# A recurrence with a two-layer MoE on one core: the second product of seven steps as seven block products, the MoE weights in fp16, and one decay sum moved to VectorE

## Chip, core and metric

The kernel runs on one core of a Trainium2 chip. The metric is device time in microseconds of one launch. The kernel before took 183.21 us (median of three runs, 183.01 to 183.66). Engines are called PE (TensorE), DVE (VectorE), ACT (ScalarE), POOL (GpSimd) and SP (SyncE, which only issues transfers).

## What is computed

For 4 batches and 8 heads of width 48, a state of 48 x 48 runs over 768 tokens. The outputs of all heads side by side are a row of 384 for each of 3072 tokens, and that row goes through two products with a squared relu between them.

```python
for t in range(S):                                   # per batch and head
    cur = outer(u * k[t], v[t])
    y[t] = r[t] @ (state + cur)
    state = w[t][:, None] * state + outer(k[t], v[t])
x = y laid out as [3072, 384]
h = x @ w_in                                         # 384 x 2048
g = maximum(h, 0) ** 2
out = g @ w_out                                      # 2048 x 384
```

All inputs and the output are fp32.

## The kernel before

**Tiling.** The work is 12 steps, three to a batch, of 256 tokens each; a partition holds two neighbouring tokens. A step has an attention part and a MoE part. In the attention part the decay is summed within chunks of 128 tokens in the log domain, the state is carried from chunk to chunk, and the products are bf16 matmuls. In the MoE part the step's 256 tokens go through the first product in 8 groups of 2 x 128 hidden units, and then through the second product in two halves of 128 tokens (`c`), each 16 matmuls of 384 columns that accumulate over the 2048 hidden units in one PSUM bank.

**The order.** Nothing is scheduled by a compiler. `ORDER` (from line 17) is a list of words, each the call of a small function; instructions are issued to their engines in the order of the words, and each engine works through its own list in order, held back by semaphores where data is not ready or a buffer not free. A word is `name.step...`; `:n` names a PSUM bank and `=A`, `=V` or `=G` the engine (ACT, DVE, POOL). PE, DVE, ACT, POOL and SP each have one queue. SP issues all loads, stores and DMA transposes.

**The words of a step**, with the line of their main instruction:

- `ld.s.x`: loads of w, r, k, v (L180); `ld.g.i` and `ld.g.o`: quarters of w_in (L188) and w_out (L193); `cast.i.g`, `cast.o.g`: their casts to bf16 (L200).
- `ww_`, `rw_`, `kw_`: products of two SBUF tiles (L267, L279, L283) on POOL or DVE. `lw_`: the logarithm (L271, ACT).
- `cum_`: the decay sums by matmuls: four of 2 columns (L311), the exclusive sum (L313) and the negated inclusive sum (L314), 384 columns each. `exp_` and `ac_` (L318, L325, ACT) take exponentials of them in PSUM.
- `rd_`: r and k times their decays (L332, DVE). They are transposed either on PE (`tr_`, L341, with the copies `rkt_`, L345) or by DMA (`dtr_`, L348).
- `p_` (L365), `pm_` (mask, L376, DVE), `su_` (L387), `ts_` (L395, L397), `sn_` (the state, L401, POOL), and `y_`, `yq_`, `yc_` (L411): the attention's products.
- `ku_`, `qp_` (L286, L291, POOL), `q_` (L294, DVE), `vq_` (L297, POOL): the term of u.
- `ysb_` (L449): eviction of y. Its transposes are `yt_` on PE (L457) with the copy `xt_` (L461), or `dyt_` by DMA (L464).
- `m1_` (L474): a group of the first product, 6 matmuls of 256 columns into one of four banks. `rl_` (relu, L481 on ACT, L483 on DVE) evicts it; `sq_` (L489 on ACT, L491 on DVE) squares four blocks of 128 hidden units in place.
- `m2_.s.c.q` (L497): a quarter of a token half of the second product, 4 matmuls of 384 columns. `os_` (L503 on ACT, L505 on DVE) evicts a half, scaled; `store` (L509).
- `warm_.n.b` (L513): n matmuls of 512 columns on zeros.

**Memory.** PSUM has two double banks (`att`) for the attention and four single banks (`one`) for the MoE and the transposes. SBUF buffers are handed on by counting uses (`buf`, line 159).

Of the kernel before, what the change touches and what calls it, by code (L numbers as in the profile page):

```python
# [29 lines left out]
cast.o.1=G rl_.1.3=V ww_.3=V vq_.2 m2_.0.1.0:3 p_.2.0:1 p_.2.1:0 sq_.1.1=A lw_.3 pm_.2.1 m2_.1.1.0:0 sq_.1.2=A  # L30
m2_.1.0.0:2 sn_.2.0 qp_.3 pm_.2.0 q_.3 rw_.3=V m2_.0.0.1 m2_.1.1.1 m2_.1.0.1 m2_.0.1.1 cum_.3:0 y_.2:1 ww_.4=G kw_.3=G
v_.3=G sq_.1.3=A cast.o.2=A yc_.2 sq_.0.2=A yq_.2 m2_.1.1.2 kw_.4=G ysb_.2=V cast.o.3=A ac_.3 exp_.3 m2_.1.0.2
m2_.0.0.2 m2_.0.0.3 m2_.1.1.3 rd_.3.0 rd_.3.1 os_.0.0=A ld.5.v ld.6.w ld.5.k lw_.4 os_.1.1=A m2_.1.0.3 os_.1.0=V
yt_.2:1 cum_.4:1 tr_.3.0:0 su_.3:0 xt_.2=A rw_.4=G tr_.3.1:2 m2_.0.1.2 m1_.2.0:1 ts_.3.0=V rkt_.3.0=V sn_.3.0 ww_.5=G
ac_.4 exp_.4 ld.7.w store.0.0 rd_.4.0 v_.4=G ku_.4 rkt_.3.1=A m2_.0.1.3 m1_.2.6:2 m1_.2.3:0 ts_.3.1=V rd_.4.1 p_.3.1:1
p_.3.0:0 vq_.3 dtr_.4.1 os_.0.1=A qp_.4 sn_.3.1 v_.5=G kw_.5=G rl_.2.3=A lw_.5 rl_.2.0=A pm_.3.1 m1_.2.1:3 m1_.2.2:0
m1_.2.5:1 pm_.3.0 su_.4:1 y_.3:0 rl_.2.1=A sq_.2.0=A dtr_.4.0 rl_.2.5=A yc_.3 yq_.3 rl_.2.6=V ysb_.3=A rl_.2.2=V
m1_.2.7:3 m1_.2.4:1 cum_.5:0 sq_.2.1=A rl_.2.7=V yt_.3:2 ts_.4.0=V rl_.2.4=V ac_.5 xt_.3=A sn_.4.0 q_.4 rw_.5=V ku_.5
sq_.2.2=A m2_.2.0.0:0 exp_.5 m2_.2.0.1 m2_.2.1.0:2 rd_.5.0 m2_.2.1.1 rd_.5.1 m2_.2.1.2 m1_.3.7:1 dtr_.5.0 m1_.3.1:3
sq_.2.3=A rl_.3.1=A dtr_.5.1 qp_.5 store.1.1 m2_.2.1.3 ts_.4.1=V p_.4.1:0 p_.4.0:1 rl_.3.7=V os_.2.1=V m1_.3.3:1  # L40
m2_.2.0.2 ld.6.r ld.6.k ld.7.r vq_.4 sn_.4.1 pm_.4.0 ww_.6=G ww_.7=G pm_.4.1 m1_.3.2:2 m1_.3.0:3 su_.5:1 y_.4:0
ts_.5.0=V q_.5 rl_.3.0=V yc_.4 ld.7.k store.1.0 ld.6.v ld.8.w yq_.4 p_.5.0:1 pm_.5.0 rl_.3.3=A rl_.3.2=A sq_.3.1=A
ysb_.4=A m1_.3.5:2 m2_.2.0.3 ku_.6 vq_.5 yt_.4:1 m1_.3.4:3 p_.5.1:1 xt_.4=V lw_.7 cum_.7:0 rl_.3.5=V os_.2.0=A lw_.6
pm_.5.1 m1_.3.6:0 m1_.4.3:1 rw_.7=V rl_.3.4=A exp_.7 sq_.3.0=A kw_.7=G sn_.5.0 cum_.6:1 m1_.4.1:3 rl_.4.3=A rl_.4.1=A
kw_.6=G rw_.6=G m1_.4.0:2 m1_.4.5:1 rl_.3.6=A m2_.3.1.0:3 m2_.3.0.0:0 exp_.6 sq_.3.2=A rl_.4.5=A sq_.3.3=A rl_.4.0=V
rd_.7.0 m2_.3.0.1 m2_.3.1.1 rd_.7.1 m2_.3.0.2 rd_.6.0 m1_.4.4:1 ww_.8=G qp_.6 rd_.6.1 ac_.7 ld.8.r ld.7.v store.2.1
dtr_.6.0 dtr_.6.1 ld.11.w ac_.6 m2_.3.0.3 m1_.4.2:2 v_.6=A v_.7=A su_.6:1 y_.5:0 yc_.5 yq_.5 q_.6 m2_.3.1.2 ysb_.5=A
ts_.6.0=A m2_.3.1.3 os_.3.1=A os_.3.0=V rl_.4.4=V rl_.4.2=V ld.9.w ku_.7 vq_.6 sn_.6.0 yt_.5:1 ld.8.k store.3.0 ld.8.v
rw_.8=V ts_.6.1=V xt_.5=A qp_.7 m1_.4.7:0 m1_.4.6:3 m1_.5.7:2 sq_.4.2=A rl_.4.6=A rl_.4.7=A rl_.5.7=V p_.6.1:1
p_.6.0:0 m1_.5.0:1 m1_.5.1:3 pm_.6.1 m1_.5.5:0 m1_.5.4:2 pm_.6.0 rl_.5.0=V lw_.8 sq_.4.0=A rl_.5.1=A sq_.4.3=A  # L50
rl_.5.5=A y_.6:1 su_.7:0 store.0.1 ld.9.k sq_.4.1=V rl_.5.4=A sn_.6.1 kw_.8=V q_.7 dtr_.7.0 yc_.6 yq_.6 m2_.4.0.0:3
m1_.5.6:2 m1_.5.3:0 m1_.5.2:1 ysb_.6=A dyt_.6 rl_.5.6=V m2_.4.1.0:2 dtr_.7.1 rl_.5.2=A v_.8=A ld.9.r ld.10.w store.3.1
ts_.7.0=V sn_.7.0 rl_.5.3=V ww_.9=V m2_.4.1.1 cum_.8:1 m2_.4.0.1 ac_.8 lw_.9 exp_.8 m2_.4.0.2 ku_.9 sq_.5.0=A
# [36 lines left out]
def kernel(  # L90
# [39 lines left out]
    def bf16_bank(i):  # L130
        return one[i][:].bitcast(BF16)
# [434 lines left out]
```

## Time and profile before

| | |
|---|---|
| median of 3 runs | 183.21 us |
| the profiled execution | 183.09 us, its span 181.3 us |
| PE busy | 174.1 us (96%), 2293 matmuls |
| DVE busy | 127.1 us (70%) |
| ACT busy | 120.0 us (66%) |
| POOL busy | 110.8 us (61%) |
| first product (L474) | 576 matmuls, 71.2 us busy |
| second product (L497) | 384 matmuls, 68.9 us busy |
| chain that ended last, by engine | PE 86% |

The profile is of one execution. Its span runs from the first to the last instruction; the 1.8 us between span and time lie around it. A matmul's row gives its duration from issue to its end, and matmuls overlap: what one costs in a stream is the distance between starts, which the chain of work shows (so many of a line in so many microseconds). In the views a group is a line of the code with its engine and operation, what it writes and reads, the number of instructions, and the mean duration in nanoseconds; "idle before" is how long the engine stood still ahead of them, and who ended it.

### The profile page before, as it was taken

To read this page: it belongs to the slowest core of one execution; us is meant where nothing else is said; L and a number is where in the kernel's file an instruction comes from. 1 tells how busy PE (TensorE), PEld (TensorE's weight loads), DVE (VectorE), ACT (ScalarE), POOL (GpSimd) and SP (SyncE) were. 2 spreads that over 40 slices of the span, in tenths; PEclk is the share of its full clock that TensorE was granted. 3 is DMA by queue.
4 is the path that set the end of the run, shared out by engine and by line. 5 is a ranking of instruction groups with operands and counts; after the bars stand their busy time and mean duration, and the time that the engine had idled before them with its cause. 6 is when DMAs were issued, how large, how long until landed. Compare 5 with 4: busy or idle time off the path is not lost.

```text
span 181.3 us, 5434 instructions
## 1 busy us (share of the span) xinstructions
PE 174.1 (96%) x2293; PEld 125.1 (69%) x2294; DVE 127.1 (70%) x176; ACT 120.0 (66%) x191; POOL 110.8 (61%) x104
## 2 busy tenths in 40 slices
PE   7978899999999999999999999999999999999992
PEld 2355689766787787777777778777666777777661
DVE  5499958947787889776967969287996718327431
ACT  5779798999788568959949384747870366528001
POOL 6389989977899977999059960999555010000000
PEclk9999999999999999999999999999999999999999
DMA  5999999998999599979999559983659821302023
GB/s 149 325 352 395 334 235 356 353 343 205 309 241 190 102 236 302 288 179 262 289 109 254 108 118 245 239 233 115 34 130 145 192 47 43 90 0 87 4 87 130
DMA packets 78810, 35.61 MB, mean 196 GB/s; under 512 B 72129, under 2 KB 77250, under 8 KB 78786
## 3 DMA queue, kind: packets, MB, share of 16 engines
q1 hardware_dynamic: 78786, 35.27, 77.6%
q8 instruction: 18, 0.29, 0.7%
q14 instruction: 6, 0.05, 0.1%
HBM read 25.17 MB, written 4.72 MB: 165 GB/s over the span
## 4 chain that ended last, share of the span: by engine, by line
PE 86%; DMA 5%; SPq 5%; issue 1%; ACT 1%
PE one L497 35%; PE one L474 34%; PE att L411 7%; DMA w_st_b<-in_moe_w_in_dram 5%; SPq L180 3%; PE att L365 3%; PE att L387 2%; SPq L188 1%; PE one L341 1%; PE att L313 1%; PE one L457 1%; PE att L314 1%; SPq L208 1%; PE att L311 0%; ACT gt_b L481 0%
## 5 line engine op out<-in xcount | busy, mean ns | idle before, releaser
L474 PE MATMUL one<-xT_b,wi_sb 128*128 128x256 bf16 x576 | 71.2, 273 | 0.7 <-ACT gt_b L481 0.5
L497 PE MATMUL one<-wo_sb,gt_b 128*128 128x384 bf16 x384 | 68.9, 326 | 0.0
L474 PEld LDWEIGHTS <-wi_sb 128*128 128x128 bf16 x576 | 55.3, 98 | 11.7 <-issue 0.9
L497 PEld LDWEIGHTS <-gt_b 128*128 128x128 bf16 x384 | 36.7, 98 | 21.7 <-ACT gt_b L489 0.2
L481 ACT ACTIVATE gt_b<-one 128x512 f16<-128x512 f32 x51 | 29.9, 596 | 24.6 <-PE one L474 24.0
L483 DVE TENSOR_SCALAR gt_b<-one 128x512 f16<-128x512 f32 x45 | 30.3, 685 | 17.0 <-PE one L474 15.7
L489 ACT ACTIVATE gt_b<-gt_b 128x1024 bf16<-128x1024 f16 x38 | 39.4, 1054 | 0.9 <-DVE gt_b L483 0.7
L401 POOL TENSOR_TENSOR S_b<-t_b,ac_buf 128x384 bf16<-128x384 f32 x20 | 17.3, 864 | 23.9 <-DVE t_b L397 17.0
L376 DVE TENSOR_TENSOR pmT_b<-att,mask 128x1024 bf16<-128x1024 f32 x22 | 26.0, 1216 | 6.2 <-PE att L365 6.2
L286 POOL TENSOR_TENSOR ku_b<-k_b,u_bc 128x768 f32<-128x768 f32 x12 | 22.8, 1910 | 3.0 <-DMA k_b<-in_k_dram 2.3
L291 POOL TENSOR_TENSOR ku_b<-ku_b,r_b 128x768 f32<-128x768 f32 x12 | 21.8, 1814 | 1.2 <-DMA r_b<-in_r_dram 1.2
L297 POOL TENSOR_TENSOR vq_b<-v_b,q_b 128x768 bf16<-128x768 f32 x12 | 18.1, 1506 | 0.4 <-DVE q_b L294 0.3
L503 ACT ACTIVATE w_st_b<-one 128x384 f32<-128x384 f32 x12 | 5.9, 490 | 16.5 <-PE one L497 16.5
L294 DVE TENSOR_REDUCE q_b<-ku_b 128x16 f32<-128x768 f32 x12 | 11.3, 946 | 4.5 <-POOL ku_b L291 4.5
L332 DVE TENSOR_TENSOR rdec_buf<-r_b,att 128x768 bf16<-128x768 f32 x12 | 11.3, 949 | 3.9 <-ACT att L318 3.8
L505 DVE TENSOR_SCALAR w_st_b<-one 128x384 f32<-128x384 f32 x12 | 6.6, 552 | 8.2 <-PE one L497 7.5
L449 ACT CAST y_sb_b<-att 128x768 bf16<-128x768 f32 x8 | 6.4, 799 | 8.0 <-PE att L411 7.8
L332 DVE TENSOR_TENSOR rdec_buf<-k_b,att 128x768 bf16<-128x768 f32 x12 | 11.3, 948 | 0.5 <-ACT att L318 0.4
L279 POOL TENSOR_TENSOR r_b<-r_b,w_b 128x384 f32<-128x384 f32 x8 | 8.1, 1014 | 3.4 <-DMA r_b<-in_r_dram 3.4
L397 DVE TENSOR_TENSOR t_b<-S_b,att 128x384 f32<-128x384 bf16 x16 | 8.8, 547 | 1.7 <-PE att L387 0.9
L318 ACT ACTIVATE att<-att 128x768 f32<-128x768 f32 x12 | 9.6, 800 | 0.5 <-PE att L314 0.3
L513 PE MATMUL one<-warm 128*128 128x512 bf16 x23 | 8.1, 490 | 1.2 <-DVE warm L235 1.2
(71 smaller groups left out, 180.0 us busy)
## 6 DMA issues: line engine op xcount, KB each, us to landing
w_b<-in_w_dram SPq DMA_DIRECT2D x12, 384.0 KB, 5.1
r_b<-in_r_dram SPq DMA_DIRECT2D x12, 384.0 KB, 5.0
k_b<-in_k_dram SPq DMA_DIRECT2D x12, 384.0 KB, 6.0
v_b<-in_v_dram SPq DMA_DIRECT2D x12, 384.0 KB, 5.2
out_dram<-w_st_b SPq DMA_DIRECT2D x24, 192.0 KB, 2.3
w_st_b<-in_moe_w_in_dram SPq DMA_DIRECT2D x4, 768.0 KB, 9.6
w_st_b<-in_moe_w_out_dram SPq DMA_DIRECT2D x4, 768.0 KB, 8.2
rkT_b<-rdec_buf SPq DMA_TRANSPOSE x16, 3.6
```

The source lines that it names most:

```text
L286: nc.gpsimd.tensor_mul(buf("ku", s)[:], buf("k", s)[:, :, 1:3, :], u_bc[:, :, None, :].to_broadcast([C, H, 2, D]))
L291: nc.gpsimd.tensor_mul(ku[:], ku[:], buf("r", s)[:, :, 0:2, :])
L297: nc.gpsimd.tensor_mul(buf("vq", s)[:].rearrange("p j h d -> p h j d"), buf("v", s)[:], buf("q", s)[:, :, :, None].to_broadcast([C, H, 2, D]))
L332: nc.vector.tensor_mul(rdec[:, i, :, :, 0:D], x.rearrange("p h j d -> p j h d"), cs[:, i, 0:DM].rearrange("p (h d) -> p h d", h=H)[:, None ...
L376: nc.vector.tensor_mul(pmT, ps_p[:].rearrange("p e (a x) -> p (e a) x", a=2), mk.to_broadcast([C, 4, 2 * C]))
L401: nc.gpsimd.tensor_mul(buf("S", s + c, 1 - c)[:], buf("t", s, c)[:].rearrange("p (a e d) -> p a e d", a=HP, e=2), tiles["a_c", s][:, :, c, ...
L411: nc.tensor.matmul(ps_y[rows, c, cols], lhsT, rhs, start=fresh, stop=True, skip_group_check=True)
L474: nc.tensor.matmul(ps1[:, j, :], wi_sb[:, n // 4, kk, n % 4 * 128:(n % 4 + 1) * 128], xT[:, :, kk, :], start=(kk == 0), stop=(kk == KT - 1))
L481: nc.scalar.activation(rl, m1, AF.Relu, scale=RS)
L483: nc.vector.tensor_scalar(out=rl, in0=m1, scalar1=RS, scalar2=0.0, op0=ALU.mult, op1=ALU.max)
L489: nc.scalar.activation(gt, rl, AF.Square)
L497: nc.tensor.matmul(m2, gt[:, n, c * C:(c + 1) * C], wo_sb[:, n, :], start=(n == 0), stop=(n == NT - 1))
```

## The change

The second product of steps 4 to 10 is done by a scheme of the Strassen and Winograd kind. The two token halves (`c`), the even and odd blocks of hidden units (`k`) and the two halves of the 384 output columns make eight block products of 8 matmuls with 192 columns. Seven products of sums replace them: `sw_` forms four sums of blocks of the squared activations for each half of the hidden units (eight instructions of 128 x 512 elements a step), `tw_` forms four sums of weight blocks once, `pw_` are the seven products, and `cx_` and `ow_` evict and combine them (three and four instructions of 192 columns a step, in place of two `os_`). Two of the sums are written over the activations they no longer need; the others and the weight sums lie in buffers that the loads of the weights have left. In a bank `wx`, products 1, 6, 7 and 4 accumulate one after the other and are read after each; in a bank `wy`, 2 stands in one half, 5 and 3 in the other.

The MoE weights are kept in fp16 in place of bf16. From step 3 the negated inclusive sum is formed by DVE from the exclusive one (`ni_`) in place of a matmul. `ORDER` is written anew: among other things step 3's r and k and step 5's y are transposed by DMA; the first w_in quarters keep their place among the loads, while w of step 2 now stands ahead of the fourth; there are 12 early `warm_` matmuls in place of 24, and 8 after the last word; and engines are given anew to many words (POOL has 21 of the 56 `sw_`, DVE 35). The new order has 40 `m2_` in place of 96, 49 `pw_`, 16 `cx_` on ACT and 5 on DVE, 25 `ow_` on DVE and 3 on ACT. The arguments `f` of `rd_`, `tr_` and `rkt_` are not used by this order.

```diff
-    wi_sb = consts.tile([C, DFF // GW, KT, GW], BF16)
-    wo_sb = consts.tile([C, NT, DM], BF16)
+    wi_sb = consts.tile([C, DFF // GW, KT, GW], FP16)
+    wo_sb = consts.tile([C, NT, DM], FP16)
...
         nc.tensor.matmul(cs[:, 0, 0:DM], tri_strict[:], lw[:, :, 0:D], start=True, stop=True)
-        nc.tensor.matmul(cs[:, 1, 0:DM], tri_incl_neg[:], lw[:, :, 0:D], start=True, stop=True)
+        if s not in by_vector:
+            nc.tensor.matmul(cs[:, 1, 0:DM], tri_incl_neg[:], lw[:, :, 0:D], start=True, stop=True)
...
+    def ni_(s):
+        cs = tiles["cs", s]
+        e, i = [cs[:, n, 0:DM].rearrange("p (h d) -> p h d", h=H) for n in range(2)]
+        nc.vector.scalar_tensor_tensor(out=i, in0=e, scalar=-1.0, in1=tiles["lw", s][:, :, 0:D],
+                                       op0=ALU.mult, op1=ALU.subtract)
...
+    half = slice(0, DM // 2), slice(DM // 2, DM)
+
+    def tw_(i):
+        b = [[wo_sb[:, k::2, cols] for cols in half] for k in range(2)]
+        t = wo_sums
+        op, x, y = [(ALU.subtract, b[0][1], b[0][0]), (ALU.subtract, b[1][1], t[0]),
+                    (ALU.subtract, b[1][1], b[0][1]), (ALU.subtract, b[1][0], t[1])][i - 1]
+        engine_of("tw_", i).tensor_tensor(out=t[i - 1], in0=x, in1=y, op=op)
+
+    def sw_(s, h, i):
+        gt = buf("gt", s)[:, 8 * h:8 * h + 8, :].rearrange("p (n k) (c t) -> p c k n t", k=2, c=2)
+        sg = None if i == 3 else buf("sg", s)[:, :, 4 * h:4 * h + 4, :]
+        out, x, y, op = {
+            1: lambda: (sg[:, 0], gt[:, 1, 0], gt[:, 1, 1], ALU.add),
+            2: lambda: (sg[:, 1], sg[:, 0], gt[:, 0, 0], ALU.subtract),
+            3: lambda: (gt[:, 1, 0], gt[:, 0, 0], gt[:, 1, 0], ALU.subtract),
+            4: lambda: (gt[:, 0, 1], gt[:, 0, 1], sg[:, 1], ALU.subtract)}[i]()
+        engine_of("sw_", s, h, i).tensor_tensor(out=out, in0=x, in1=y, op=op)
+
+    def pw_(s, i):
+        where_to = {1: lambda: wx(s), 6: lambda: wx(s), 7: lambda: wx(s), 4: lambda: wx(s),
+                    2: lambda: wy(s, 0), 5: lambda: wy(s, 1), 3: lambda: wy(s, 1)}[i]()
...
+        for n in range(NT // 2):
+            nc.tensor.matmul(where_to, gt[:, n, :], wo[:, n, :], start=(n == 0 and i in (1, 2, 5)),
+                             stop=(n == NT // 2 - 1), skip_group_check=True)
+
+    def cx_(s, i):
+        scaled(("cx_", s, i), buf("xz", s)[:, (i - 1) % 2, :], wy(s, 1) if i == 3 else wx(s))
+
+    def ow_(s, i):
+        o_sb = buf("o", s, (i - 1) // 2)[:, half[(i - 1) % 2]]
+        if i == 3:
+            scaled(("ow_", s, i), o_sb, wx(s))
+        else:
+            x, more = {1: (wy(s, 0), 0), 2: (wy(s, 1), 1), 4: (wx(s), 0)}[i]
+            nc.vector.scalar_tensor_tensor(out=o_sb, in0=x, scalar=1.0 / (RS * RS), in1=buf("xz", s)[:, more, :],
+                                           op0=ALU.mult, op1=ALU.add)
```

`scaled` is a scaled copy out of PSUM by ACT or DVE. A piece of the new order, around steps 6 to 8:

```
sw_.6.1.1=V yq_.8 sq_.7.1=A yc_.8 rl_.7.6=V sw_.6.0.1=V sw_.6.0.2=V m1_.7.0:3 pw_.6.1:1 rl_.7.4=A ts_.9.0=A dtr_.9.1
sw_.6.1.2=V ww_.11=V sw_.6.0.3=V qp_.9 sn_.9.0 dtr_.9.0 ysb_.8=A ts_.9.1=V sw_.6.1.3=G cx_.6.1=V dyt_.8 pw_.6.2:0
rl_.7.5=A p_.9.1:1 sw_.6.1.4=G q_.9 p_.9.0:0 rl_.7.0=A pw_.6.6
```

224 lines of the change are left out of this document (139 added, 85 removed).

## The prediction

> **What bounds the kernel now.** I read the page's shares first, then the chain that ended last in order of time, then busy time by windows, then a piece of the timeline.
>
> ```profile
> span 181.3 us, 5434 instructions
> ...
> PE 174.1 (96%) x2293; PEld 125.1 (69%) x2294; DVE 127.1 (70%) x176; ACT 120.0 (66%) x191; POOL 110.8 (61%) x104
> ...
> PE   7978899999999999999999999999999999999992
> ...
> PEclk9999999999999999999999999999999999999999
> ```
>
> From the sixth slice (22.7 us) to the last TensorE is busy in every slice, at full clock. The chain says whether that is the path:
>
> ```profile
> 10.80 9.58 DMA w_st_b<-in_moe_w_in_dram
> ...
> 31.26 0.45 PE one L341 x8
> ...
> 40.15 0.16 PE att L314
> ...
> 41.56 4.01 PE one L497 x24
> ...
> 45.57 0.33 PE one L457 x6
> ...
> 83.12 1.97 PE one L474 x18
> ...
> 168.90 9.11 PE one L497 x56
> 178.01 0.02 issue
> 178.03 0.49 ACT w_st_b L503
> ```
>
> From 22.43 us to 178.01 the chain is TensorE without a break, so a microsecond of matmul taken out there comes off the end, if nobody else becomes late. Before it stands the transfer of the third quarter of w_in (lands at 20.39), after it an eviction and a store. The pitches that I use follow: the second product (L497) 4.01/24 = 0.167 us by this line and 9.11/56 = 0.1627 in the long run, the first (L474) 1.97/18 = 0.109, a transpose 0.45/8 = 0.056. By columns, 384, 256 and 128 cost 162.7, 109 and 56 ns: 0.417 ns a column and some 2.5 ns.
>
> **What the change takes from TensorE.** (a) 14 token halves of four quarter products, 56 x 4 matmuls of 384 columns: 56 x 0.651 = 36.5 us out. In: 7 steps x 7 blocks x 8 matmuls = 392 of 192 columns, 192 x 0.417 + 2.5 = 82.5 ns each, no row has this width: 32.3 us. Gain 4.1. (b) Nine of twelve inclusive sums (L314), 0.16 each: 1.4. (c) The two transpose groups of step 3 (0.45 each) and step 5's (0.33) become DMA transposes: 1.2. Sum 6.8 us (rounding). Fewer warm-up matmuls early lie beside transfers; the eight at the very end (0.21 us each, 1.7) lie beside the last eviction and store, which take 181.3 - 178.0 = 3.3.
>
> ```profile
> L497 PEld LDWEIGHTS <-gt_b 128*128 128x128 bf16 x384 | 36.7, 98 | 21.7 <-ACT gt_b L489 0.2
> ```
>
> A weight load lasts 98 ns, longer than a 192-column matmul. Were loads not to overlap each other, a block matmul would cost 98: 392 x 15.5 ns = 6.1 us back. The transposes also load 128 x 128 weights each time and run every 56 ns, so loads do overlap; I take 82.5 and keep 98 as a rival. The Trainium skill (TensorE: Matmul & The Clock Gate, "LDWEIGHTS") prices a load at its columns over 1.2 GHz, 107 ns for 128, and would make the gain of (a) a loss of 5.5 us; the 56 ns here speak against it. fp16 weights in a matmul appear in no row: between nothing and the double that the fp32 bias product shows per pass (0.55 us against 0.33 at 384 columns, two passes); I take nothing, all being two-byte operands (the double would add over 90 us and need no further sum).
>
> **What it adds elsewhere.** A DVE instruction's successor starts some 0.085 us before it ends (below: 93.00 + 0.81 against a next start at 93.73), so I count mean less 0.085 (0.05 on POOL, 0.1 on ACT).
> - sw_, 56 sums of 128x512 two-byte elements: 35 on DVE, 21 on POOL. DVE: half of a 1024-element square (L491, 0.68), 0.34 to 0.68; a pitch of 0.33 is taken. POOL: between 384 elements (1.01) and 768 (1.81) lies 1.27; 1.2 taken.
> - ow_ and cx_, 49 evictions of 192 columns for 14 of 384 (0.55 DVE, 0.49 ACT): half of those to all of them; 0.265 DVE, 0.23 ACT taken.
> - ni_, nine, like L397 (0.547): 0.47. tw_, four of 1536 elements: 1.5 squares, 0.86.
> None is on TensorE's path by itself: they lie beside 6 to 8 us of other matmuls a step. Each block chain holds TensorE's queue, though: the sixth block adds to the bank that cx_ has just read, so the first block's cx_ must be done. Mostly 1.2 to 2 us of matmuls lie between (step 6: second block and p_); in step 8 only the second block (0.66), against 0.6 of a relu queued ahead on ACT and 0.33 of cx_: some 0.3 late. On POOL a sw_ waits for squares of ACT, and behind it stand ku_, vq_ and sn_ of the next steps, which y_ needs; that queue has 6 us of room only where POOL now waits.
>
> The first transpose of step 3 by DMA takes 3.6 us (median to landing) behind rd_; 5.6 us of matmuls are written between. If that cover were gone, TensorE would wait up to 3.6. The two issues (1.27 each on SP) stand ahead of store.0.0 and the loads of steps 4 to 6, which are used over 5 us later.
>
> Start: the third w_in quarter keeps its place and its bytes in the queue, so its cast again ends near 21.9. Before, four first-product groups (0.655 each) came ahead of it in TensorE's queue, now two: 1.3 late, less the 0.5 that TensorE then still waited for a relu (22.43). The earlier k and r of step 0 may give some back. +0.8 taken, 0 to +2 (the fourth quarter now lies behind w of step 2, 1.1 us).
>
> **Where DVE and POOL meet.**
>
> ```profile
> 92.56 0.83 POOL L401 TENSOR_TENSOR S_b<-t_b,ac_buf 128x384 bf16<-128x384 f32 x1 [6.27 <-DVE t_b L397]
> ...
> 93.00 0.81 DVE L267 TENSOR_TENSOR ww_b<-w_b 128x384 f32<-128x384 f32 x1
> ...
> 93.35 2.13 POOL L286 TENSOR_TENSOR ku_b<-k_b,u_bc 128x768 f32<-128x768 f32 x1
> ```
>
> L267 takes 0.56 when POOL is idle. Here it is 0.25 longer: it ends 0.42 after POOL's S_b, and POOL's next takes 2.13 instead of 1.81. It happens to every DVE instruction with two SBUF inputs that meets a POOL instruction under way: L279 at 58.5, 71.7 and 82.0 took 0.18, 0.74 and 0.51 more than its 0.55, L491 at 118.9 took 0.28 more; where POOL was idle (88.6, 89.2, 111.6, 131.8) none. PSUM inputs (L397, L376) never show it. The Trainium skill (SBUF — State Buffer, "SBUF: two separate sides") calls it an exclusive lock for whole instructions, and the trace agrees (0.25 and 0.32 here).
>
> ```profile
> sum 50.00, PE 50.00 PEld 37.55 DVE 38.02 ACT 37.53 POOL 37.69; mean PE 10.00 PEld 7.51 DVE 7.60 ACT 7.51 POOL 7.54
> ```
>
> That is before, 70 to 120 us, with 6 such DVE instructions. The like stretch of the new order (after m2_.3.1.3 to m1_.9.0), 50 us of matmuls, sums to DVE 47.2, POOL 44.4, ACT 42.5, and 39 such instructions on DVE, 15.2 us of its time; 44.4 + 15.2 = 59.6 if POOL and they exclude each other. (The same sum over before's words from 70.4 to 120.4 us of matmuls gives DVE 37.5, beside the 38.0 shown.) So DVE comes near TensorE. From 35 to 133 us before, 12 such instructions lost 2.0 us together, 0.167 each: 39 x 0.167 = 6.5, DVE 53.7, 3.6 us over TensorE. Bounds: nothing, if they fall into POOL's gaps, and 0.39 each, the mean of the five that met POOL: 47.2 + 15.3 - 50 = 12.4. I take 3.6. Outside that stretch DVE has room (22 of the last 40 us).
>
> **Sum.** 183.09 (span 181.3 and 1.8 around it) - 6.8 + 0.8 + 3.6 = **180.7 us**; the median before, 183.21, lies 0.1 above its profiled run.
>
> **Rivals.**
> - Clean gain: the sums fall where POOL waits, as it does 17 us in total for t_b (L401's idle time). For it: TensorE now has 0.7 us of stalls with DVE at 70%. 183.1 - 6.8 + 0.8, with up to 1.5 of small stalls: 176.5 to 178.6. 0.28.
> - Gain eaten: bank waits and late sums cost TensorE some 6 us: 182.4 to 184. For it: from pw_.4.1 to ow_.4.3 the new order holds two of the four banks over 15 us of matmuls, so the relus of the first product get less slack. 0.12.
> - Slower: DVE and POOL exclude each other in the 70 to 120 stretch at 0.39 a meeting, and DVE sets the pace: 180.7 - 3.6 + 12.4 = 189.5. It turns the sign where stalls pass 6.0: (50 + 6.0 - 47.2)/39 = 0.23 us each. For it: 59.6 us of mutually exclusive work in 50. Against: 7 of 12 before lost next to nothing. 0.15, anywhere from 184 to 190.
> - Weight loads set the block pace (98 ns): 180.7 + 6.1 = 186.8. 0.03.
> - Forecast, 178.6 to 182.4: 0.42.
>
> **Chances.** A measurement tells 0.3% (0.55 us) from no change. Faster: 0.42 + 0.28 + 0.02 of the eaten = 0.72; same: 0.08; slower: 0.02 + 0.15 + 0.03 = 0.20. Range 176.8 to 186.5: it leaves out a little of the clean gain (0.05) and the far end of the slower ones (0.12).
>
> **What would show it.** Block matmuls at 82 ns in the chain (98 or more: loads). DVE's sw_ rows with a median of 0.35 and a mean above 0.5: meetings; POOL instructions 0.3 longer beside them. In the chain, breaks between 90 and 150 us that end at DVE or POOL rows are the 3.6; breaks at cx_ are bank waits; no breaks, the clean gain. TensorE's first unbroken stretch should begin some 0.8 us later in its order than now. A chain that runs through DVE for more than 10 us proves the forecast wrong, as does a start lost to a slow clock in the 20 us with few warm-ups.

## The result, and the profile after

The kernel after takes **192.31 us** (median of 4 runs, 191.54 to 193.55), the kernel before 183.44 beside it: ratio 1.0499, 95% interval [1.0447, 1.0551]. The prediction said 180.7, faster. The sign is wrong, and the time lies above the range. An execution that took over 1.5% longer than the fastest of its kernel stays in the medians below but is left out of the ratios (six of ten in e2) and, where it is the profiled one (e10, e11), out of the table's columns from the profile.

The page of the kernel after, the lines that answer to those of before:

```profile
span 190.1 us, 5807 instructions
...
PE 172.8 (91%) x2425; PEld 135.4 (71%) x2427; DVE 149.2 (78%) x231; ACT 130.2 (68%) x218; POOL 135.3 (71%) x123
...
PE   7678799979999899989964999999879999999996
...
PEclk9956999999999999999997899999999999999999
```

TensorE's row is no longer full: there are eights and nines with holes in the middle (`64`, `87`), and the clock row has two dents, one at 10 to 17 us and one near 102 us. The rest is read from one stretch: from the first matmul of the second product to TensorE's last useful one, so that the start and the course behind it come apart. First before, then after (columns: stretch and length, then the busy time of each engine and its instructions, the granted clock, DMA share, GB/s):

```profile
33.84:178.01 144.17, 144.16 (x1896) 104.67 (x1894) 101.26 (x136) 92.42 (x145) 83.12 (x68) 1.00 0.74 172
```

```profile
36.27:186.65 150.38, 140.82 (x2033) 114.56 (x2033) 121.87 (x190) 102.67 (x171) 106.80 (x85) 0.99 0.69 166
```

Before, TensorE is busy for 144.16 of 144.17 us. After, it begins 2.4 us later (36.27 against 33.84), has 3.3 us less to do, and stands idle for 9.6 us. The whole difference of the two profiled executions, 192.04 - 183.09 = 8.95 us, is 2.43 (start) - 3.34 (busy) + 9.55 (idle) + 0.3 (what lies behind the stretch and around the span).

The largest of the breaks, 4.33 us, in the timeline (start, duration, engine, line, what; in brackets the idle time before and its releaser):

```profile
95.03 0.56 DVE L304 TENSOR_TENSOR k_b<-k_b,w_b 128x384 f32<-128x384 f32 x1 [1.84 <-DMA k_b<-in_k_dram]
95.08 2.18 POOL L307 TENSOR_TENSOR ku_b<-k_b,u_bc 128x768 f32<-128x768 f32 x1 [2.35 <-DMA k_b<-in_k_dram]
...
95.51 2.04 DVE L568 TENSOR_TENSOR w_st_b<-w_st_b,gt_b 128x512 bf16<-128x512 bf16 x1
...
97.22 1.65 POOL L318 TENSOR_TENSOR vq_b<-v_b,q_b 128x768 bf16<-128x768 f32 x1
97.46 1.96 DVE L530 TENSOR_TENSOR gt_b<-gt_b 128x1024 bf16<-128x1024 f16 x1
...
98.84 1.28 POOL L440 TENSOR_TENSOR S_b<-t_b,ac_buf 128x384 bf16<-128x384 f32 x1
99.35 1.58 DVE L555 TENSOR_TENSOR w_st_b<-wo_sb 128x1536 f16<-128x1536 f16 x1
...
102.12 0.42 DVE L568 TENSOR_TENSOR w_st_b<-w_st_b,gt_b 128x512 bf16<-128x512 bf16 x1
...
102.60 1.62 PE L590 MATMUL one<-w_st_b,w_st_b 128*128 128x192 f16 x9 [4.33 <-DVE w_st_b L568]
```

kw_.8 on VectorE and ku_.8 on GpSimd wait for the same transfer (k of step 8) and start together, at 95.03 and 95.08. From there the two engines take turns: each VectorE instruction with two SBUF inputs starts while a GpSimd product (ku_, vq_, then sn_) is under way and ends after it by nearly its own length (0.29, 0.55 and 0.81 us). The sum takes 2.04 us where the same form takes 0.42 at 102.12, the square 1.96 where its shortest is 0.68, tw_.3 1.58 where 0.95. Three such waits, 3.5 us, stand ahead of sw_.4.0.2 at 102.12, and the sixth block product of step 4 (pw_.4.6) waits for it. The clock answers to the break (same columns as above, 1 us each):

```profile
102.00:103.00 1.00, 0.40 (x3) 0.39 (x4) 1.00 (x3) 0.00 (x0) 0.00 (x0) 0.72 0.90 217
103.00:104.00 1.00, 1.00 (x8) 0.95 (x7) 1.00 (x5) 0.00 (x0) 0.00 (x0) 0.50 0.99 247
104.00:105.00 1.00, 1.00 (x9) 0.94 (x8) 1.00 (x5) 0.33 (x1) 0.00 (x0) 0.50 1.14 334
105.00:106.00 1.00, 1.00 (x8) 0.80 (x6) 0.96 (x4) 0.00 (x0) 0.51 (x1) 0.57 1.13 342
```

The granted clock is 0.5 for 3.4 us behind the break, so it costs another 1.7. The Trainium skill (TensorE: Matmul & The Clock Gate, "What's actually happening") gives half the clock after an idle window of about 3.4 us; the trace agrees for this break.

A second place of the same kind ends at 142.70. There the chain that ended last runs through VectorE (start, duration, what):

```profile
135.14 0.60 DVE gt_b L522
135.74 0.47 DVE r_b L300
136.21 0.27 DVE w_st_b L609
136.47 0.84 DVE k_b L304
137.31 1.73 DVE rdec_buf L370 x2
139.04 0.27 DVE w_st_b L597
139.31 1.74 DVE sg_b L568
...
142.70 1.49 PE one L590 x16
...
145.11 0.67 PE one L590 x8
```

7.5 us of the path are VectorE's, with one sum at 1.74 (0.42 alone). Most of it is VectorE's own work; the waits for GpSimd in it are some 1.8 us (this sum, and kw_.10 at 136.4, 0.92 in the timeline for 0.55). The last line shows the block products at the expected pace: eight in 0.67 us.

### The profile page after: what moved, and what is told of

The parts are those of the page before. It is cut to its first block, busy times and chain, and to the rows that moved or that the text cites. A ratio compares the mean times of both kernels' runs of the same rounds, so it can differ in the third digit from the quotient of the medians.

```text
span 190.1 us, 5807 instructions
## 1 busy us (share of the span) xinstructions
PE 172.8 (91%) x2425; PEld 135.4 (71%) x2427; DVE 149.2 (78%) x231; ACT 130.2 (68%) x218; POOL 135.3 (71%) x123
## 5 line engine op out<-in xcount | busy, mean ns | idle before, releaser
L513 PEld LDWEIGHTS <-wi_sb 128*128 128x128 f16 x576 | 55.1, 98 | 11.7 <-issue 3.7
L528 ACT ACTIVATE gt_b<-gt_b 128x1024 bf16<-128x1024 f16 x42 | 43.3, 1056 | 5.6 <-DVE gt_b L522 5.4
L520 ACT ACTIVATE gt_b<-one 128x512 f16<-128x512 f32 x60 | 35.1, 596 | 16.1 <-PE one L513 15.8
L536 PE MATMUL one<-wo_sb,gt_b 128*128 128x384 f16 x160 | 29.3, 326 | 0.0
L522 DVE TENSOR_SCALAR gt_b<-one 128x512 f16<-128x512 f32 x36 | 24.3, 686 | 3.8 <-PE one L513 2.6
L590 PEld LDWEIGHTS <-gt_b 128*128 128x128 bf16 x280 | 23.6, 98 | 1.9 <-issue 0.8
L536 PEld LDWEIGHTS <-gt_b 128*128 128x128 bf16 x160 | 15.1, 98 | 8.7 <-issue 0.3
L590 PE MATMUL one<-wo_sb,gt_b 128*128 128x192 f16 x168 | 16.7, 246 | 0.1
L590 PE MATMUL one<-w_st_b,gt_b 128*128 128x192 f16 x112 | 11.5, 246 | 0.2 <-DVE w_st_b L609 0.2
L590 PE MATMUL one<-w_st_b,w_st_b 128*128 128x192 f16 x64 | 7.4, 276 | 4.3 <-DVE w_st_b L568 4.3
L488 ACT CAST y_sb_b<-att 128x768 bf16<-128x768 f32 x10 | 8.0, 798 | 4.1 <-PE att L450 3.9
```

The source lines that it names most:

```text
L513: nc.tensor.matmul(ps1[:, j, :], wi_sb[:, n // 4, kk, n % 4 * 128:(n % 4 + 1) * 128], xT[:, :, kk, :], start=(kk == 0), stop=(kk == KT - 1))
L520: nc.scalar.activation(rl, m1, AF.Relu, scale=RS)
L522: nc.vector.tensor_scalar(out=rl, in0=m1, scalar1=RS, scalar2=0.0, op0=ALU.mult, op1=ALU.max)
L528: nc.scalar.activation(gt, rl, AF.Square)
L536: nc.tensor.matmul(m2, gt[:, n, c * C:(c + 1) * C], wo_sb[:, n, :], start=(n == 0), stop=(n == NT - 1))
L590: nc.tensor.matmul(where_to, gt[:, n, :], wo[:, n, :], start=(n == 0 and i in (1, 2, 5)), stop=(n == NT // 2 - 1), skip_group_check=True)
```

## Experiments

Theories named in the expectations: **A**, the time is lost where VectorE's two-input instructions meet GpSimd's products (ku_, qp_, vq_, "the u products") ahead of TensorE, and to the half clock behind; **B**, VectorE simply has too much to do; **C**, the start, ni_ or fp16; **D**, GpSimd is late, not in the way; **E**, the sums cost the same in every step. **F** and **G** came later and concern the chain of seven blocks.

The table holds each run's time, and from its profile the stretch from the first matmul of the second product to TensorE's last useful one. "met" is of the whole profile: how many VectorE instructions of two SBUF inputs took over 0.05 us more than the shortest of their line, and how many us all of them together took over it.

| kernel | us, median | ratio to before | first m2_ | stretch | idle in it | met |
|---|---|---|---|---|---|---|
| before | 183.2 | 1 | 33.8 | 144.2 | 0.0 | 5, 2.1 |
| after | 192.3 | 1.050 | 36.3 | 150.4 | 9.6 | 13, 10.4 |
| e1 sums first | 191.2 | 1.042 [1.038, 1.046] | 37.6 | 147.9 | 8.7 | 15, 12.1 |
| e2 no u | 184.9 | 1.000 [0.995, 1.005] | 35.1 | 142.7 | 3.7 | 9, 3.9 |
| e3 before, no u | 183.1 | 0.999 [0.996, 1.002] | 33.9 | 144.2 | 0.0 | 2, 0.7 |
| e4 eight products | 187.3 | 1.020 [1.016, 1.025] | 37.6 | 144.5 | 1.8 | 9, 6.9 |
| e5 sums and vq_.7 moved | 191.9 | 1.048 [1.043, 1.054] | 37.7 | 148.5 | 7.5 | 13, 9.7 |
| e6 memsets for u | 186.9 | 1.020 [1.017, 1.023] | 35.7 | 146.2 | 5.0 | 8, 4.0 |
| e7 no ni_ | 193.1 | 1.055 [1.050, 1.060] | 36.4 | 151.6 | 8.8 | 13, 10.5 |
| e8 more warm-ups | 193.3 | 1.053 [1.047, 1.059] | 35.4 | 151.8 | 10.2 | 15, 10.0 |
| e9 seven late | 186.7 | 1.016 [1.008, 1.023] | 36.2 | 145.4 | 4.4 | 13, 8.2 |
| e10 seven early | 193.6 | 1.049 [1.039, 1.059] | | | | |
| e11 no sums | 190.5 | 1.034 [1.025, 1.042] | | | | |
| e12 eight, no u | 185.4 | 1.010 [1.003, 1.018] | 36.9 | 144.8 | 2.1 | 4, 1.4 |
| e13 no sums, no u | 183.8 | 1.003 [1.001, 1.006] | 36.1 | 142.4 | 3.6 | 4, 1.6 |
| e14 no reads in the chain | 190.8 | 1.044 [1.040, 1.047] | 36.4 | 148.9 | 8.2 | 17, 12.0 |
| e16 before, fp16 code | 183.2 | 1.002 [0.999, 1.005] | 34.1 | 144.3 | 0.1 | 5, 1.7 |
| e15 before, seven late | 191.4 | 1.046 [1.043, 1.049] | 34.1 | 152.2 | 7.4 | 12, 9.7 |
| e17 mended | 188.8 | 1.031 [1.029, 1.033] | 33.5 | 150.7 | 4.6 | 12, 6.3 |
| e18 mended twice | 185.0 | 1.012 [1.007, 1.016] | 33.7 | 146.2 | 2.7 | 10, 5.6 |

### Is it the u products, and where?

**e1**, the three sums ahead of kw_.8 in VectorE's list (words of the order, shortened):

```diff
+ sw_.4.1.2=V sw_.4.0.1=V sw_.4.0.2=V
  kw_.8=V
```

> Only the order of five DVE instructions changes: the three sums sw_.4.1.2, sw_.4.0.1 and sw_.4.0.2 stand ahead of kw_.8 (which waits for a transfer), sq_.5.0 and tw_.3. Theory A (the loss sits at meetings of two-input DVE instructions with POOL, above all at the one place where pw_.4.6 waited 4.33 us, after which the clock stood at half for 3.4 us and cost some 1.7 more): the gap and the half clock go, 192.3 - 6 = 186 to 188 us. Theory B (DVE has too much work, whatever the order; the lateness comes up at the next place): at most 1.5 us better, 190.8 or more.

191.23, where B put it and 3 us above A. The sums are at their shortest, but the same three GpSimd instructions now meet the next three of VectorE's (sq_.5.0 2.30, tw_.3 2.23, rw_.8 1.18), and the break comes at the next block, 3.53 us, ended by ow_.4.1 behind them. They lose the same as those in after, 1.62, 1.27 and 0.63 us over the shortest, within 0.01. A's "place" was too narrow: the meeting moves to whatever follows in the list.

**e2** and **e3**, GpSimd's u products left out (the output lacks the u term) in after and in before:

```diff
-        nc.gpsimd.tensor_mul(buf("ku", s)[:], buf("k", s)[:, :, 1:3, :],
-                             u_bc[:, :, None, :].to_broadcast([C, H, 2, D]))
+        buf("ku", s), buf("k", s)
```

> The changed kernel without POOL's three products of the u term (ku_, qp_, vq_: the output lacks the u term; q_ on DVE and yq_ on TensorE still run, on zeros). POOL loses some 62 us, DVE and TensorE keep all their work. Theory A (meetings with POOL): hardly any DVE instruction is lengthened, the sum of what they take over their shortest falls from 10.4 us to under 3, and the time falls by the 8 us of TensorE gaps that I trace to meetings, to 183 to 186 us. Theory B (DVE's own load): DVE's queue is as long as before, 189 us or more.

> The control: the kernel before without the same three products of POOL (the output lacks the u term). TensorE had no gaps there after 22 us, so both theories expect no change: 182.7 to 183.9 us. If it gains, e2's gain is not that of meetings.

e2: 184.93 by the median of ten runs between 181.9 and 186.7. That is 7.4 us less than after by the medians and 9.1 by the ratios (1.0499 and 1.0002); A said 183 to 186, B 189 or more. What VectorE's instructions lose falls to 3.9 us, not under 3. e3: 183.07, ratio 0.9993 [0.9963, 1.0023]: the kernel before loses no time that can be measured to the same products. The same piece of VectorE's list in e2:

```profile
93.91 0.42 DVE L567 TENSOR_TENSOR w_st_b<-w_st_b,gt_b 128x512 bf16<-128x512 bf16 x1
94.25 0.69 DVE L529 TENSOR_TENSOR gt_b<-gt_b 128x1024 bf16<-128x1024 f16 x1
94.85 0.95 DVE L554 TENSOR_TENSOR w_st_b<-wo_sb 128x1536 f16<-128x1536 f16 x1
```

0.42, 0.69 and 0.95, for 2.04, 1.96 and 1.58.

**e6**, GpSimd as busy, but not reading: each u product is one element a partition (it keeps the wait) and memsets about as long (the output lacks the u term).

```diff
-        nc.gpsimd.tensor_mul(ku[:], ku[:], buf("r", s)[:, :, 0:2, :])
+        nc.gpsimd.tensor_mul(ku[:, 0:1, 0, 0:1], ku[:, 0:1, 0, 0:1], buf("r", s)[:, 0:1, 0, 0:1])
+        for heads in (H, H, 3):
+            nc.gpsimd.memset(ku[:, 0:heads], 0.0)
```

> The kernel after with GpSimd's products ku_, qp_ and vq_ written as a product of one element a partition (which keeps the wait) and two or three memsets about as long (1.85, 1.85 and 1.5 us), so the output lacks the u term. GpSimd is as busy as in the kernel after but reads almost nothing from SBUF in these instructions. If the two engines exclude each other while both read SBUF (theory A): as the kernel without the u products, 183 to 186, with at most 6 us of lengthened VectorE instructions. If it was only that GpSimd's other results came late, since these products hold its queue (theory D): 189 to 192, with VectorE's instructions at their shortest times. If a memset holds VectorE up as a product does: 190 to 193 and over 9 us lengthened.

186.91: by the medians 5.4 of e2's 7.4 us go, by the ratios 5.5 of 9.1, though GpSimd's busy time in the stretch is as high as in after (110.1 us against 106.8). It is nearest to A, 0.9 above its range; D's 189 and the 190 of "a memset holds VectorE up" are out. The other 2 to 3.6 us are left for D, and the trace shows one place of that kind:

```profile
78.30 1.95 POOL L300 TENSOR_TENSOR r_b<-r_b,w_b 128x384 f32<-128x384 f32 x2
79.33 0.95 DVE L376 TENSOR_TENSOR rdec_buf<-r_b,att 128x768 bf16<-128x768 f32 x1 [3.64 <-POOL r_b L300]
...
81.80 0.52 PE L519 MATMUL one<-xT_b,wi_sb 128*128 128x256 bf16 x2 [2.80 <-DVE gt_b L528]
```

rw_.6 stands behind the memsets in GpSimd's list, rd_.6 waits for it, a relu waits behind rd_.6, and TensorE for the relu: 2.80 us. Reading makes the difference, as the Trainium skill says (SBUF — State Buffer, "Who interferes with whom"): a GpSimd instruction that only writes SBUF does not contend.

**e5**, the sums and tw_.3 ahead of kw_.8, and vq_.7 ahead of ku_.8 on GpSimd (words, shortened):

```diff
+ vq_.7 sw_.4.1.2=V tw_.3=V sw_.4.0.1=V sw_.4.0.2=V
  kw_.8=V
```

> On VectorE's list the three sums of step 4 and tw_.3 stand ahead of kw_.8, which waits for a transfer, and on GpSimd's list vq_.7 stands ahead of ku_.8, which waits for the same transfer, so that GpSimd's three products no longer run side by side with the sums. Theory A (the lost time is meetings of the two engines that happen to lie on TensorE's path, and the half clock behind the long break): the 4.3 us break and the half clock behind it go, no break over 1.5 us is left between 85 and 110 us; 185 to 188. Theory B (VectorE has too much to do in this stage, in whatever order): the breaks come back elsewhere, 190 to 193. Theory C (start, ni_, fp16): 191 to 193.

191.88, as B and C said. The breaks near 100 us fall from 4.33 to 0.49 and 2.04, and the stretch is 1.9 us shorter, but two of the moved sums meet again (1.68 with vq_.7, 2.03 with ku_.8), and this execution started 1.4 us later. Two orders made by hand moved the meetings and did not take them away.

### ni_, the start, fp16

**e7**, the twelve inclusive sums on TensorE again (all ni_ words removed):

> The kernel after with its twelve inclusive sums on TensorE again, as one matmul more in each cum_. TensorE's work grows by 1.4 us, VectorE's falls by 4 to 5. Theory A: the break at 98 us stays, since no ni_ is among what the sums of step 4 met; 190.5 to 193. Theory B (too much work on VectorE): 187 to 189. Theory C with ni_ as the cause: 186 to 188.

193.05, the upper end of A's range. VectorE has 3.7 us less in its stretch (118.2 against 121.9) and it brings nothing. That speaks against B, as do e2, which leaves VectorE all its work, and e11 below, which takes 12.8 us of it away (109.1 against 121.9) and is still at 190.5.

**e8**, ten more warm-ups between 6 and 20 us:

> The kernel after with ten more idle matmuls on zeros in the first 20 us. If the half clock from 10 to 16 us is what makes the start late: the clock there is 1.0, the first m2_ starts by 35.3 us in place of 36.3, and the time falls by 0.5 to 1.5 us, to 190.8 to 191.8. If the start is late for the transfers and casts of the weights alone: first m2_ at 36.0 to 36.5, and 192 to 192.6. In both the break at 98 us stays.

193.3: a miss. The clock is mended and the first m2_ is earlier (35.4), but nothing of it reaches the end. The mean granted clock from 10 to 20 us was 0.66 in after; here:

```profile
10.00:20.00 10.00, 7.50 (x174) 4.59 (x172) 9.74 (x14) 8.16 (x11) 9.84 (x8) 1.00 1.07 356
```

TensorE loses behind the start what it gained ahead of it: idle is 10.2 for 9.6 us, with new breaks of 1.68 at 88.8, which ends at an eviction by ScalarE, and of 1.92 at 117.6, which ends at a DMA transpose. Nor does e8 show that the clock makes the start late: e4 has the same start, a granted clock of 1.00 from 10 to 20 us and its first m2_ at 37.6, while e2 has 0.66 and 35.1.

**e16**, the order of before in the code of after (fp16 weights, eight products):

> The order of the kernel before in the code of the kernel after: the MoE weights in fp16, eight products in every step, no ni_. If fp16 costs nothing, as the 82.5 ns of a block matmul say: 182.8 to 183.7.

183.23, ratio 1.002 [0.9993, 1.0046]. fp16 costs nothing that this can tell.

### Eight or seven, early or late

**e4**, after with eight quarter products in place of the seven blocks, no sums:

```diff
- pw_.4.1:0 cx_.4.1=A ... pw_.4.2:1 ... pw_.4.6 ...
+ m2_.4.1.0:0 ... m2_.4.0.0:1 ... m2_.4.1.1 ...
```

> The new order with eight block products again: each step's seven pw_ are replaced in place by the quarter products m2_, and sw_, tw_, cx_ and ow_ are dropped (os_ stands where the last ow_ of a half stood). fp16 weights, ni_ and the new start stay. TensorE has 4.1 us more. Theories A and B: the gaps that come from the sums go, those at cum_.3 (1.3) and at step 3's and 7's transposes (0.5 each) and the later start (2) stay: 192.3 + 4.1 - 10 = 186 to 187.5 us. Theory C (the new order's start, ni_ and fp16 are to blame, not the sums): 191 us or more.

187.27; C's 191 is out. Its stretch is 144.5 us, that of before: with eight products the new order loses its time at the start alone (3.8 us in this profile). Seven for eight adds 5.0. The same three GpSimd instructions meet three of VectorE's here too, and take 1.62, 1.28 and 0.64 us from them (sq_, rw_.8, ww_.9; the first is shown), but TensorE then stops for 1.04 us, not 4.33:

```profile
94.48 2.30 DVE L522 TENSOR_TENSOR gt_b<-gt_b 128x1024 bf16<-128x1024 f16 x1
...
100.30 0.81 PE L505 MATMUL one<-xT_b,wi_sb 128*128 128x256 bf16 x6 [1.04 <-DVE gt_b L514]
```

What differs is not the meeting but what TensorE needs from behind it.

**e12**, the same without u:

> The new order with eight products (187.3) and without GpSimd's u products, so the output lacks the u term. With it the four kernels eight or seven, with or without u, are complete: 187.3, 192.3, this one, 184.9. Theory A: with eight products only 1.5 us of breaks come from VectorE, so this gains at most that, 185.8 to 187.5, and seven products are ahead of eight once GpSimd's products are gone. Rival: the new order is as dear for its u products with eight as with seven, 181 to 184, and seven products gain nothing even without them.

185.4, 0.4 below what A said. Seven for eight costs 5.0 us with the u products. Without them it gains 0.5 by the medians and 1.8 by the ratios (1.0102 and 1.0002, whose intervals overlap).

**e9** and **e10**, seven in steps 8 to 10 or in 4 to 7 only (words of e4 in the other steps):

> The order of the kernel after with eight products in steps 4 to 7 and seven only in steps 8 to 10, whose sums lie behind 145 us, where VectorE and GpSimd have room. Measured for the order with eight in all seven steps: 187.3. Theory A (seven products gain 0.585 us a step, and lose it where their sums meet GpSimd's products ahead of TensorE): 185.3 to 186.8. Theory B (VectorE has too much to do, but only up to 145 us): the same. Theory E (the sums cost as much in every step, 5.0 / 7 = 0.7 net): 189 to 190.

> The mirror: seven products in steps 4 to 7 and eight in steps 8 to 10. Theories A and B: all of the loss stays, and the gain of three steps is missing: 192 to 194.5. Theory E: 4 x 0.7 over 187.3, 189.5 to 191.

186.74 and 193.57. All of the loss is in steps 4 to 7; E's 189.4 is out. Late, three steps of seven gain 0.5 us by the medians over e4, not 1.75, and that is not clear of the noise.

### The sums or the chain of blocks?

**e11**, after with the sums left out (the second product is of wrong terms; zeros are written once):

```diff
-        engine_of("sw_", s, h, i).tensor_tensor(out=out, in0=x, in1=y, op=op)
+        if i == 1 and s in (4, 5):
+            nc.vector.memset(sg, 0.0)
```

> The kernel after without its sums (sw_ and tw_ write nothing but a few zeros, so the second product of steps 4 to 10 is of the wrong terms), while the 28 half-size block products, the scaled copies and the additions to the outputs stay. If the sums on VectorE and GpSimd are what costs (A and B): the four blocks' gain comes out whole, 187.3 - 4.1 = 183.2, so 182 to 184.5, with fewer than 7 us of lengthened VectorE instructions. If the waits of the chain of blocks for their banks (cx_, ow_) are the cost: 187 to 190.

190.5, ratio 1.034. **The theory that the sums cost falls**: without them at most a third of the 9 us comes back (1.8 us by the medians, 3.0 by the ratios), and the time lies 0.5 above the range that the expectation gave for the waits of the chain. The durations of VectorE and GpSimd in its trace show why, with the sums gone:

```profile
135.53 1.80 POOL L312 TENSOR_TENSOR ku_b<-ku_b,r_b 128x768 f32<-128x768 f32 x1
135.66 2.09 DVE L300 TENSOR_TENSOR r_b<-r_b,w_b 128x384 f32<-128x384 f32 x1
...
137.29 2.12 POOL L307 TENSOR_TENSOR ku_b<-k_b,u_bc 128x768 f32<-128x768 f32 x1
...
137.94 1.89 DVE L304 TENSOR_TENSOR k_b<-k_b,w_b 128x384 f32<-128x384 f32 x1
```

rw_.10 and kw_.10 take 2.09 and 1.89 for 0.55. In after the same two products met one sum (1.81). So the loss does not go by how many instructions of VectorE can be met: 22 such instructions in e4 lost 6.9 us, 61 in after 10.4. It does not go by GpSimd's products alone either: the kernel before has the same u products and lost 2.1.

**e13**, neither sums nor u products (both edits above), and **e14**, the reads in the middle of the chain left out (cx_ and two of four ow_ write nothing, the others copy a bank once; wrong terms), sums and u kept:

```diff
-        scaled(("cx_", s, i), buf("xz", s)[:, (i - 1) % 2, :], wy(s, 1) if i == 3 else wx(s))
+        buf("xz", s)
```

> The kernel after without its sums and without GpSimd's u products: the second product of steps 4 to 10 is of the wrong terms and the u term is missing. Taking away the sums alone left 190.5, the u products alone 184.9. Theory F (the chain of seven blocks has so little slack that any late VectorE instruction stops TensorE, and it is the meetings with GpSimd's products that make them late, the sums' or others'): both away give at most what the u products away gave, 181 to 184.5. Theory G (the chain's own waits for its banks cost, meetings or not, and the sums add little): 188 to 190.

> The kernel after without the reads in the middle of the chain of blocks: cx_ and two of the four ow_ write nothing, the other two copy a bank each once, as os_ did, so the second product of steps 4 to 10 is of the wrong terms. All sums and all u products stay. Theory F: each block has one wait less, but pw_.4.6 waits for sw_.4.0.2 as before; 185 to 189. Theory G: 183 to 185. If the sums' own waits are all there is to it (theory A): 190 to 192.5.

e13: 183.81, within F's figures and clear of G's. It is 1.1 us below e2 by the medians and no faster by the ratios (1.0033 and 1.0002), so a cost of the sums once u is gone is not shown. e14: 190.81, above what F and G said and where A put it: the same three instructions take the same 2.04, 1.96 and 1.58, the break is as long, and the reads in the chain are not what TensorE waits for:

```profile
94.62 2.04 DVE L568 TENSOR_TENSOR w_st_b<-w_st_b,gt_b 128x512 bf16<-128x512 bf16 x1
...
96.58 1.96 DVE L530 TENSOR_TENSOR gt_b<-gt_b 128x1024 bf16<-128x1024 f16 x1
...
98.46 1.58 DVE L555 TENSOR_TENSOR w_st_b<-wo_sb 128x1536 f16<-128x1536 f16 x1
...
101.71 1.62 PE L590 MATMUL one<-w_st_b,w_st_b 128*128 128x192 f16 x9 [4.29 <-DVE w_st_b L568]
```

Taking out sums alone or reads alone leaves 190 to 191; taking out the u products leaves 184 to 185, with or without the sums.

### A version that gains?

**e15**, **e17**, **e18**: the order of before, and from step 8's second product on a tail written anew with seven products in steps 8 to 10, m1_ and pw_ in turn:

```diff
- m2_.8.0.0:3 ... m2_.8.0.1 m2_.8.0.2 ... m1_.9.5:1 m1_.9.4:2 ... m2_.8.0.3
+ pw_.8.1 cx_.8.1=A pw_.8.2 ... m1_.9.5 ... pw_.8.6 cx_.8.2=A m1_.9.4 pw_.8.5
```

> The order of the kernel before up to step 8's second product, and behind it a tail of its own with seven products in steps 8, 9 and 10, where GpSimd has no u products left: half of the sums on VectorE, half on GpSimd, block products and m1_ in turn. fp16 weights, no ni_, the start of before. The three steps' gain is 3 x 0.585 = 1.75 us. Theories A, F: 181.2 to 182.6. Theory G (the chain costs by itself): 183 to 185.

191.37, a miss of 9 us. I had put two tw_ on GpSimd:

```profile
130.89 3.10 POOL L550 TENSOR_TENSOR w_st_b<-wo_sb 128x1536 f16<-128x1536 f16 x1
...
132.11 2.42 DVE L525 TENSOR_TENSOR gt_b<-gt_b 128x1024 bf16<-128x1024 f16 x1
...
133.94 3.53 POOL L550 TENSOR_TENSOR w_st_b<-wo_sb,w_st_b 128x1536 f16<-128x1536 f16 x1
...
134.92 3.10 DVE L525 TENSOR_TENSOR gt_b<-gt_b 128x1024 bf16<-128x1024 f16 x1
```

Two squares of 0.68 took 2.42 and 3.10, TensorE stood still for 3.94 us, and the half clock followed: the same mechanism again, brought in by my own choice of the engine.

**e17**, tw_ and all sums on VectorE:

> The order of before with seven products in steps 8 to 10 once more, with what the first try showed mended: all four tw_ and all sums on VectorE (there two tw_ of 3.1 and 3.5 us on GpSimd held two sq_ of VectorE up by 1.7 and 2.4 us, and TensorE by 3.9), the stores of step 7 ahead of step 8's, ScalarE's squares of step 10 between its copies of step 11. GpSimd has nothing from the sums. Theory F: the three steps' 1.75 us less what the chain loses at its banks: 181.4 to 183.0. If the chain of seven costs by itself even with GpSimd quiet: 184 to 187.

188.84. GpSimd has nothing from the sums, and yet there are two breaks of 1.58 and 1.74 us. os_.7.1 and an ow_ of step 8 waited for output buffers whose stores had not landed:

```profile
142.45 0.49 ACT L537 ACTIVATE w_st_b<-one 128x384 f32<-128x384 f32 x1 [4.20 <-DMA out_dram<-w_st_b]
...
145.13 0.36 DVE L604 SCALAR_TENSOR_TENSOR w_st_b<-one,w_st_b 128x192 f32<-128x192 f32 x1 [2.01 <-DMA out_dram<-w_st_b]
```

**e18**, against e17 three buffers more and two tw_ later:

```diff
-    free["o"], free["sg"] = [], []
+    free["o"], free["sg"] = [consts.tile([C, DM], FP32, name=f"o_b{i}") for i in range(3)], []
```

> The run before with its two breaks mended: three output buffers more (os_ and ow_ of steps 7 and 8 waited for stores; the second buffers for the sums and the scaled copies are given up for them, since the three steps follow one another), and tw_.3 and tw_.4 behind 140 us, where VectorE is idle. The breaks of 1.6, 1.7 and 0.9 us and the half clock behind them go. Theory F: 181.3 to 183.3. If the chain of seven costs by itself: 184 to 187.

184.99: slower than before by 1.2%, above F's 183.3 and within what was said for a chain that costs by itself. Its 2.7 us of idle all lie between 141.4 and 149.5 us, in step 8, behind one more meeting (a sum of 1.58 beside vq_.11) and pw_ that wait for sums; from 150 to the end TensorE is busy without a break. No version beats the kernel before.

## Why the prediction was wrong, point by point

- **"So many microseconds out of TensorE: 6.8".** Right as work. The block products run at 0.67/8 = 84 ns where 82.5 was said, and neither weight loads (98 ns) nor fp16 cost anything (e16). The busy time of the stretch fell by only 3.3: 1.8 of the rest is the half clock (after's 140.8 against 139.0 in e2), and a group that stops at its end is drawn some 0.16 us longer than its pace in a stream (0.82 against 0.66); whether that makes up the remaining 1.7 was not counted.
- **"+0.8 taken" for the start, "0 to +2".** Too small: 2.4 here, 1.2 to 3.9 over the profiles of the new order in the table. The slow clock that the last sentence of the prediction named is there (0.66 from 10 to 20 us), but that it makes the start late is not shown: the first m2_ came 0.9 us sooner with it mended in e8 and 1.4 later at full clock in e4. The cause of the late start stays open. It is nearly all of what the new order costs with eight products (e4: 3.8 of 4.3 us; e12).
- **"39 x 0.167 = 6.5, DVE 53.7, 3.6 us over TensorE".** This is the step that failed. Its terms came out; taking the longer of two loads for the time did not. The stretch of that sum is 88.02 to 147.30 us in after. There the 39 instructions lost 7.3 us (6.5 said) and VectorE was busy for 53.0 (53.7 said), yet the stretch took 59.3. TensorE stood idle for 7.1 us of it and VectorE for 6.3: neither set the pace throughout. I had added the loss to VectorE's load as if it were spread thin and the 2.8 us of room could take some. It comes in a few lumps of 0.2 to 1.6 us, and where one stands ahead of the sum that the next block product needs, TensorE stops: the three in a row at 95 to 101 us make up most of the 4.33 us break, behind which come 1.7 us of half clock. Without the u products, or with memsets in their place, the same 39 instructions fit into 51.7 and 52.2 us. Over the whole course 9.6 us of idle and 1.8 of half clock stand in place of the 3.6; without the u products 3.7 of idle are left. The columns of that stretch in after, e2 and e6:

```profile
88.02:147.30 59.28, 52.23 (x814) 45.45 (x814) 52.96 (x88) 42.58 (x76) 40.61 (x33) 0.97 0.75 173
```

```profile
86.69:138.43 51.74, 50.40 (x814) 44.17 (x813) 47.72 (x88) 41.92 (x76) 18.61 (x19) 1.00 0.85 198
```

```profile
89.80:141.97 52.17, 50.64 (x813) 44.14 (x814) 47.28 (x88) 41.94 (x76) 40.31 (x60) 1.00 0.86 197
```

- **"0.167 each"** held by luck. Before, 5 of 12 instructions met GpSimd and lost 0.39 each; in after's stretch 7 of 39 did and lost 1.0 each. What one loses is what the GpSimd product still has to run: the three of the timeline started with 1.75, 1.41 and 0.77 us of it left and were late by 1.62, 1.27 and 0.63. (53.7 less 50 is 3.7, not 3.6; nothing hangs on it.)
- **"Breaks ... at DVE or POOL rows are the 3.6; breaks at cx_ are bank waits".** Of after's breaks over 0.4 us from 40 us on, five end at VectorE's rows and two at DMA transposes behind rd_, none at cx_; e14 confirms that the chain's reads matter little here.
- **"A chain that runs through DVE for more than 10 us proves the forecast wrong".** It ran through VectorE for 7.5 us in one piece. The sign was wrong all the same: a wait need not lie on the last chain in one long piece to cost.
- **The slower rival** (DVE and POOL exclude each other, 189.5, chance 0.15) had the mechanism and the sign and is 2.8 us short of the time, by a wrong price: 0.39 for every instruction and VectorE as the pace, against 0.17 and lumps. The eaten gain's mechanism, banks held too long, is not what happened in steps 4 to 7 (e14).

What stays open: 1.5 us of idle that seven products have beyond eight even without u and sums (e13 against e12); the late start; and why seven products gain only 0.5 us in e9 and 0.5 to 1.8 without u (e12 against e2), where TensorE has 1.75 and 4.1 less to do: idle there is 4.4 and 3.7 us, and not every break was followed. How much of e2's gain is GpSimd's shorter queue and not its reading is bounded by e6 alone, at 2 to 3.6 us.

## What to carry to other kernels

A wait that a queue adds is to be priced where it falls, as so many instructions ahead of the one that the bounding engine needs next, not as load against the length of a stage. Before work is moved to VectorE, look which GpSimd instructions read SBUF at that time. Here each held the VectorE instruction of two SBUF inputs that came during it until its end, whichever that was; two reorderings moved the loss (e1, e5), and a GpSimd that was idle or only wrote took most of it away (e2, e6). Here a TensorE without a single gap was worth more than 6.8 us less work on it.

## What the runs showed of the hardware

- VectorE and GpSimd alternate. In after all 13 VectorE instructions of two SBUF inputs that start with more than 0.14 us of a GpSimd product still to run end late, by what is left less 0.13 to 0.14 us; the four with less left are at their shortest. GpSimd's next one then takes longer in turn (1.65 us at 97.22, 1.47 alone). Three of VectorE's met three of GpSimd's in a row.
- A memset on GpSimd, though as long, does not hold VectorE up: in e6 16 such VectorE instructions start beside a memset and none takes over 0.02 us more than its shortest, while 7 of the 12 that start beside a product are late.
- The length of a break alone does not decide the half clock. In e8 one of 1.92 us (117.59 to 119.52) was followed by it, but one of 2.23 us (98.73 to 100.96) was not, nor was the one of 3.53 us in e1 (to 103.69). The idle window of about 3.4 us that the Trainium skill states (TensorE: Matmul & The Clock Gate, "What's actually happening") is longer than the first of these breaks and shorter than the last; the measurement decides. e8 behind the 1.92 us and behind the 2.23, then e1:

```profile
120.00:121.00 1.00, 1.00 (x19) 0.78 (x8) 0.79 (x1) 0.00 (x0) 0.41 (x1) 0.81 1.13 357
121.00:122.00 1.00, 1.00 (x7) 0.67 (x6) 1.00 (x2) 0.89 (x2) 0.00 (x0) 0.50 1.16 329
```

```profile
101.00:106.00 5.00, 4.97 (x77) 4.34 (x78) 4.00 (x11) 2.22 (x5) 2.14 (x2) 1.00 1.00 280
```

```profile
103.70:110.00 6.30, 6.30 (x97) 5.71 (x97) 5.20 (x10) 3.59 (x7) 4.27 (x5) 1.00 1.04 279
```
